# Causal attention and maxout FFN on one core: the written engine order becomes a priority

## The chip, the cores and the metric

The kernel runs on one core of a Trainium2 chip. The time is device microseconds of that core for one execution; before the change it is 972.1 us (median of 3 runs, 967.75 to 972.37). Five engines work side by side: TensorE (PE, with its weight loads as PEld), VectorE (DVE), ScalarE (ACT), GpSimd (POOL) and SyncE (SP, which here only issues DMAs). Each has one queue of instructions, fixed when the program is built, and an instruction waits at the head of its queue until the semaphores that it needs are there.

## The reference

The kernel computes causal attention with a decay bias for 8 batches of 8 heads (576 positions, head size 64), and then a feed-forward layer with a maximum over three up-projections:

```
scores = q @ k.T / sqrt(64)
cum    = cumsum(max(s, 0))
scores = where(causal, -1e9, scores + min(-(cum_q - cum_k), 0))
attn   = exp(scores - max(scores));  attn = attn / (sum(attn) + 1e-9)
x      = (attn @ v)                      # to 4608 tokens x 512
h      = max(x @ w1, x @ w2, x @ w3)     # 512 -> 768
out    = h @ w_out                       # 768 -> 512
```

The weights arrive as 64-bit floats and are decoded in the kernel. Products that need more than half precision are done as sums of parts: a high and a low part of each operand, three matmuls in place of one.

## The kernel before, in words

**Attention.** Heads are taken in pairs; a pair of one batch is a *visit*, and a block of 128 queries of a visit is a *step*. Batches 0 and 1 are visited twice, first for query blocks 0 and 1, then for blocks 2 to 4; batches 2 to 7 are visited once, for all five. That makes 160 steps. One step `t` goes through four functions, each on other engines:

- `scores(t)` (L359): PE writes the scores of both heads into a PSUM tile `s`. There are two such tiles (L64), so step `t+2` needs the tile of step `t` back.
- `highest(t)` (L445): DVE takes the row maximum `nm`.
- `expo(t)` (L451): ACT takes the exponential in place and the row sums `se`.
- `probs(t)` (L466): DVE takes the reciprocal `ri` (L480), ACT writes the high part `prh` (L496), DVE the low part `prl` (L499), which is the last reader of the score tile; then SP issues the transposing DMAs of both parts (L502, or L508 and L512 for the last block).

`values(v, ph)` (L534) multiplies the transposed probabilities with V on PE once the blocks 0 and 1 (`ph` 0) or 2 to 4 (`ph` 1) of a visit are done; its result goes to the tiles `x` (ACT L562, DVE L563).

**FFN.** When four visits have filled the `x` of one batch and half, `add_set` (L665) queues 18 groups `h_group` (12 matmuls each, L679, three of them per block of 128 hidden units) and 4 groups `o_group` (18 matmuls each, L721). A group accumulates in one of three PSUM tiles `m` (L66). The first product of a block is copied out by ACT (L693), the other two are maximised into it by DVE (L696); then ACT (L685) and POOL (L686) split it into `hh` and `hl`.

**Preparation.** Heads are loaded by SP (L121) and split into high and low parts (L150 to L168), V is scaled and split (L346, L351). The 24 weight tiles are loaded, decoded on ACT and DVE (`decode1`, `decode2`, L589 to L593), measured with small matmuls (`gram1`, L603), and then written as half-precision parts (`decode3` L647, `decode4` L652). The scale of the up weights needs all 18 of them, so the FFN can't begin before that.

**What sets the order.** The Python program emits all of this in one order. The main loop (L877 to L905) is a software pipeline by hand: in the round of step `t` it emits `probs(t)` in two parts, `highest(t+1)` between them, at most one FFN group, `scores(t+2)`, `expo(t+1)`, then what the tables `todo` and `early` hold for this step (loads, preparation, decoding), more FFN groups, and the `values` of the step before. How many groups a round takes is set by a budget: each step adds `STEP_NS` = 4800 ns less the step's own PE cost (L878), and each group takes off its cost (L752). Evacuations of a group are held back in `pending` and `later` until `drain` and `flush`.

All of it stands inside `manual_schedule()` (L67): every engine issues its instructions in exactly the order in which the program emits them. Tile buffers are handed out in that order too. The program is built with `schedule_with_timeline_sim=True` (L965).

Of the kernel before, what the change touches and what calls it, by code (L numbers as in the profile page):

```python
# [21 lines left out]
def kernel(  # L22
# [41 lines left out]
    ps_s = ctx.enter_context(tc.tile_pool(name="ps_s", bufs=2, space=PSUM))  # L64
    ps_av = ctx.enter_context(tc.tile_pool(name="ps_av", bufs=1, space=PSUM))
    ps_m = ctx.enter_context(tc.tile_pool(name="ps_m", bufs=3, space=PSUM))  # L66
    ctx.enter_context(tc.manual_schedule())  # L67


    visits = [(b, g, qbs) for qbs in ((0, 1), (2, 3, 4)) for b in range(NB) for g in range(NP)]  # L70
# [898 lines left out]
```

## Time and profile before

| | before |
|---|---|
| time, median of 3 runs | 972.1 us |
| span of the profiled execution (first to last instruction) | 972.4 us |
| highest of the three runs | 972.37 us |
| PE busy | 847.3 us, 87% |
| ACT busy | 599.1 us, 62% |
| DVE busy | 589.2 us, 61% |
| POOL busy | 285.2 us, 29% |
| mean granted clock of PE | 0.944 of full speed |

The profiled execution spans 972.4 us, and its own time is that of the highest of the runs shown, 972.37 us: nothing measurable lies around the span. Busy shares are means over a long ramp, a steady stretch and a tail that have different limits, so the prediction reads them by stage. A row of the views of waits names the instruction that waited, what released it, the microseconds in total, how often and the longest. In a timeline the number in brackets is how long the engine had been idle before the instruction, and who released it.

### The profile page before, as it was taken

What the parts mean: (1) busy time and instruction counts of PE and PEld (TensorE: products, weight loads), DVE (VectorE), ACT (ScalarE), POOL (GpSimd) and SP (SyncE); (2) the same over time, 40 slices, a digit from 0 to 9 for tenths busy, and PEclk for the clock granted to TensorE, in tenths of its full rate; (3) what the DMA queues carried; (4) which work ended last, traced back from release to release, by engine and by line L of the source; (5) the groups of instructions that cost most, each with busy time, mean ns of one, the idle gap of its engine ahead of it and who ended that gap; (6) DMA issues with size and microseconds to landing.
All of it is one profiled execution on the core that took longest, in us unless ns stands there. A gap on an engine that the chain in (4) does not pass through costs nothing. (4 is left out here: it accounts for less than half of the span.)

```text
span 972.4 us, 19924 instructions
## 1 busy us (share of the span) xinstructions
PE 847.3 (87%) x7192; PEld 658.6 (68%) x7192; DVE 589.2 (61%) x1216; ACT 599.1 (62%) x1598; POOL 285.2 (29%) x455
## 2 busy tenths in 40 slices
PE   2547759997889967999999998999999999999998
PEld 2435547775557746876788777877787778777876
DVE  6898876656546665656666566665666666554111
ACT  4657566565547676676667676666676676765121
POOL 2001221212333432333333433444343433320101
PEclk9756979999889978999999999999999999999999
DMA  8952245477467777676868676875867776734000
GB/s 299 261 149 61 82 89 128 109 134 141 93 134 145 132 159 134 126 151 117 155 115 151 120 159 111 151 140 121 150 114 143 130 156 115 140 66 97 5 24 28
DMA packets 242035, 122.34 MB, mean 126 GB/s; under 512 B 217808, under 2 KB 226512, under 8 KB 241936
## 3 DMA queue, kind: packets, MB, share of 16 engines
q1 hardware_dynamic: 237904, 108.74, 56.8%
q10 hardware_dynamic: 4032, 12.32, 4.1%
q8 instruction: 57, 0.93, 0.4%
q14 instruction: 42, 0.34, 0.2%
HBM read 60.18 MB, written 9.44 MB: 72 GB/s over the span
## 5 line engine op out<-in xcount | busy, mean ns | idle before, releaser
L679 PE MATMUL pm<-x,w 128*128 128x256 f16 (+1 forms) x3456 | 461.0, 290 | 10.9 <-DVE x L563 5.6
L679 PEld LDWEIGHTS <-w 128*128 128x128 f16 x3456 | 335.0, 99 | 99.3 <-issue 11.5
L499 DVE SCALAR_TENSOR_TENSOR prl<-s,ri,prh 128x512 f16<-128x512 f32 (+3 forms) x288 | 153.0, 568 | 109.4 <-ACT prh L496 75.5
L686 POOL TENSOR_TENSOR hl<-m,hh 128x256 f16<-128x256 f32 (+1 forms) x96 | 73.9, 770 | 459.8 <-ACT hh L685 429.8
L496 ACT ACTIVATE prh<-s,ri 128x512 f16<-128x512 f32 (+3 forms) x288 | 141.6, 538 | 41.5 <-DVE ri L480 31.3
L457 ACT ACTIVATE s<-s,nm 128x512 f32<-128x512 f32 (+4 forms) x288 | 150.9, 524 | 9.7 <-DVE nm L447 5.5
L721 PE MATMUL po<-hh,w 128*128 128x256 f16 (+1 forms) x768 | 153.0, 290 | 3.1 <-ACT hh L685 3.0
L696 DVE SCALAR_TENSOR_TENSOR m<-pm,m 128x256 f32<-128x256 f32 (+1 forms) x192 | 87.2, 454 | 106.3 <-PE pm L679 91.7
L447 DVE TENSOR_REDUCE nm<-s 128x1 f32<-128x576 f32 (+4 forms) x160 | 127.7, 798 | 37.0 <-PE s L382 24.4
L721 PEld LDWEIGHTS <-w 128*128 128x128 f16 x1152 | 111.9, 99 | 33.7 <-issue 5.5
L721 PE MATMUL po<-hl,w 128*128 128x320 f16 (+1 forms) x384 | 111.2, 290 | 1.6 <-POOL hl L686 1.6
L685 ACT ACTIVATE hh<-m 128x256 f16<-128x256 f32 (+1 forms) x96 | 42.3, 440 | 105.3 <-DVE m L696 105.3
L562 ACT ACTIVATE x<-av 128x256 f16<-128x256 f32 (+1 forms) x64 | 26.3, 411 | 78.4 <-PE av L552 78.3
L693 ACT ACTIVATE m<-pm 128x256 f32<-128x256 f32 (+1 forms) x96 | 38.9, 405 | 52.6 <-PE pm L679 52.4
L168 POOL TENSOR_TENSOR l<-raw,h 64x576 fp32r<-64x576 f32 x48 | 67.9, 1414 | 2.3 <-ACT h L154 0.7
L376 PE MATMUL s<-h 128*128 128x128 f32 (+1 forms) x192 | 54.9, 368 | 15.1 <-DVE prl L499 11.8
L563 DVE SCALAR_TENSOR_TENSOR x<-av,x 128x256 f16<-128x256 f32 (+1 forms) x64 | 29.1, 454 | 64.1 <-ACT x L562 64.1
L137 POOL CAST l<-kb 64x576 fp32r<-64x576 f32 x48 | 31.9, 666 | 113.0 <-PE s L391 100.7
L552 PEld LDWEIGHTS <-vh 128*64 128x64 f16 x832 | 45.0, 114 | 22.3 <-issue 13.4
L552 PE MATMUL av<-ph,vh 128*64 128x320 f16 (+3 forms) x384 | 57.9, 293 | 2.3 <-DMA ph<-prh 2.3
L729 ACT ACTIVATE o<-po,os 128x256 f32<-128x256 f32 (+1 forms) x64 | 31.9, 498 | 45.1 <-PE po L721 28.6
L552 PE MATMUL av<-pl,vh 128*64 128x320 f16 (+3 forms) x384 | 57.1, 285 | 2.8 <-DMA pl<-prl 2.5
(138 smaller groups left out, 1108.8 us busy)
## 6 DMA issues: line engine op xcount, KB each, us to landing
raw<-in_qk_dram SPq DMA_DIRECT2D x96, 304.0 KB, 4.8
r<-in_w_dram ACTq DMA_DIRECT2D x20, 512.0 KB, 4.8
rv<-in_qkv_dram SPq DMA_DIRECT2D x32, 320.0 KB, 3.3
out_dram<-o SPq DMA_DIRECT2D x32, 160.0 KB, 2.2
out_dram<-o SPq DMA_DIRECT2D x32, 128.0 KB, 2.2
raw<-in_qkv_dram SPq DMA_DIRECT2D x8, 480.0 KB, 3.8
ph<-prh SPq DMA_TRANSPOSE x192, 3.3
pl<-prl SPq DMA_TRANSPOSE x192, 2.8
```

The lines of the kernel that those rows point to most:

```text
L168: nc.gpsimd.tensor_tensor(out=l[far, QP:V0], in0=raw[far, QP:V0], in1=h[far, QP:V0].bitcast(F32), op=ALU.subtract)
L376: nc.tensor.matmul(ps[:, j, :nk], lhsT=w[:, qs], rhs=w[:, QP:QP + nk], start=(x == "h"), stop=False, skip_group_check=True,)
L447: nc.vector.tensor_reduce(out=nm, in_=sc, axis=AX.X, op=ALU.max, negate=True)
L457: nc.scalar.activation(out=sc, in_=sc, func=AF.Exp, bias=nm[:, j:j + 1], accum_out=sm[:, j:j + 1])
L496: nc.scalar.activation(out=hi, in_=src, func=AF.Copy, scale=sc)
L499: nc.vector.scalar_tensor_tensor(out=lo, in0=src, scalar=sc, in1=hi, op0=ALU.mult, op1=ALU.subtract)
L552: nc.tensor.matmul(av[j * D:(j + 1) * D, c0:nq], lhsT=lt, rhs=rt, start=(n < 2), stop=(n >= len(todo) - 2), skip_group_check=True,)
L679: nc.tensor.matmul(pm[:, :nq], lhsT=w[:, wt, kt, :], rhs=xt, start=(n == 0), stop=(n == 3 * NKT - 1))
L685: nc.scalar.activation(out=st["hh"][:, ft, :nq], in_=m1[:, :nq], func=AF.Copy)
L686: nc.gpsimd.tensor_tensor(out=st["hl"][:, ft, :nq], in0=m1[:, :nq], in1=st["hh"][:, ft, :nq], op=ALU.subtract)
L696: nc.vector.scalar_tensor_tensor(out=m1[:, :nq], in0=pm[:, :nq], scalar=HSC, in1=m1[:, :nq], op0=ALU.mult, op1=ALU.max)
L721: nc.tensor.matmul(pm[:, :nq], lhsT=W[18 + ft][:, wt, dt, :], rhs=st[ht][:, ft, :nq], start=(n == 0), stop=(n == 3 * NFT - 1),)
```

## The change

One line goes:

```diff
--- before.py
+++ after.py
@@ -64,7 +64,6 @@
     ps_s = ctx.enter_context(tc.tile_pool(name="ps_s", bufs=2, space=PSUM))
     ps_av = ctx.enter_context(tc.tile_pool(name="ps_av", bufs=1, space=PSUM))
     ps_m = ctx.enter_context(tc.tile_pool(name="ps_m", bufs=3, space=PSUM))
-    ctx.enter_context(tc.manual_schedule())
```

No operation is added or removed, no shape, engine or buffer count changes, and the Python program emits the same instructions in the same order. What changes is what the order means. Without the region, the framework's scheduler plays the program through against its own model of the engines' times; whenever an engine is free in that model, it takes the earliest emitted instruction whose inputs are there and whose output tile has a free buffer. The outcome is again one fixed order for each engine, with semaphores between them. On the chip, an engine still can't pass over an instruction that waits.

This holds for all queues: the matmuls on PE, the elementwise work on DVE, ACT and POOL, and the DMA issues on SP and on ACT (L186, L96, L111).

## The prediction

> **What bounds the kernel now.** I read the page first, then the busy time by stage, then PE's waits in each stage, because a mean over 972 us hides three limits.
>
> ```profile
> span 972.4 us, 19924 instructions
> PE 847.3 (87%) x7192; PEld 658.6 (68%) x7192; DVE 589.2 (61%) x1216; ACT 599.1 (62%) x1598; POOL 285.2 (29%) x455
> PEclk9756979999889978999999999999999999999999
> ```
>
> ```profile
> core 0: us, PE busy (x) PEld busy (x) DVE busy (x) ACT busy (x) POOL busy (x), PEclk, DMA share, GB/s
> 0.00:80.00 80.00, 34.64 (x256) 27.29 (x257) 64.63 (x154) 45.09 (x128) 10.87 (x36) 0.74 0.74 221
> 80.00:160.00 80.00, 61.23 (x514) 48.12 (x512) 64.37 (x127) 53.30 (x133) 14.00 (x16) 0.83 0.35 83
> 160.00:410.00 250.00, 214.29 (x1770) 161.82 (x1770) 148.69 (x295) 156.56 (x408) 75.68 (x113) 0.92 0.68 133
> 410.00:893.00 483.00, 463.53 (x4064) 363.30 (x4063) 299.10 (x614) 328.82 (x896) 175.32 (x276) 1.00 0.69 130
> 893.00:972.00 79.00, 73.58 (x594) 58.05 (x593) 12.40 (x28) 15.36 (x35) 9.29 (x14) 0.98 0.10 25
> ```
>
> PE is idle 45.4 us in the ramp (80 less 34.64), 18.8 in the second stage, 35.7 in the third, 19.5 in the steady stretch and 5.4 in the tail: 125 us in all. In the ramp DVE is the busy engine (64.63 of 80). From 410 us on PE is, at 96% and at full clock. What PE waits for there and in the third stage (the waits of PE alone, first from 160 to 410 us, then from 410 to 893 us):
>
> ```profile
> PE s L436 <- DVE prl L499: 13.4, 5, 4.3
> PE s L391 <- DVE prl L499: 7.0, 3, 3.6
> PE s L376 <- DVE prl L499: 2.8, 3, 1.9
> ```
>
> ```profile
> PE s L376 <- DVE prl L499: 9.1, 14, 1.0
> PE pm L679 <- DVE x L563: 4.7, 4, 1.2
> PE s L391 <- DVE prl L499: 4.1, 4, 1.0
> PE av L552 <- DMA pl<-prl: 0.3, 1, 0.3
> ```
>
> One wait leads everywhere: scores of step t+2 wait for the low part of step t, the last reader of the score tile. In the steady stretch it shows 18 times, 13.2 us together, 0.73 us each, and never longer than 1.0. The rows below (groups of DVE, then one of ACT, in this stretch alone; the last numbers before the second bar are busy us and mean ns) say that it has 95 steps (the reciprocal is one per step), so a step takes 483/95 = 5.08 us and four steps in five show no such wait.
>
> ```profile
> L696 DVE SCALAR_TENSOR_TENSOR m<-pm,m 128x320 f32<-128x320 f32 (+1 forms) x109 | 49.8, 457 | 41.0 <-PE pm L679 31.2 <-POOL hl L686 4.2 <-issue 2.6
> L159 DVE SCALAR_TENSOR_TENSOR h<-raw,h 64x640 fp32r<-64x640 f32 x35 | 31.1, 890 | 0.6
> L351 DVE SCALAR_TENSOR_TENSOR vl<-rv,inv,vh 128x640 f16<-128x640 f32 x19 | 20.4, 1072 | 0.0
> L480 DVE RECIPROCAL ri<-se 128x2 f32<-128x2 f32 (+1 forms) x95 | 15.1, 159 | 33.2 <-ACT se L461 32.5
> ```
>
> **The change part by part.** Nothing is removed or added, so busy time stays: PE has 847 us of work in either order. The sum is over PE's idle time by stage, and it is made against the profiled execution's 972.4 us, which is 0.3 us over the median of the runs.
>
> *Ramp, 0 to 80 us.* The FFN waits for the up weights, and those for DVE. Being free to pass over a waiting instruction helps here. The timeline of DVE and ACT around the first split weights:
>
> ```profile
> 74.24 0.40 DVE L447 TENSOR_REDUCE nm<-s 128x2 f32<-128x256 f32 x1
> 74.29 2.03 ACT L647 ACTIVATE w<-r,swu 128x512 f16<-128x512 f32 x3 [2.30 <-DVE swu L629]
> 77.62 0.88 DVE L499 SCALAR_TENSOR_TENSOR prl<-s,ri,prh 128x256 f16<-128x256 f32 x2 [2.98 <-ACT prh L496]
> ```
>
> DVE stands 2.98 us for a low part of a step, while the first high parts of the weights are being written and their low parts (L652) could follow. More than DVE's idle time in the stage, 15.4 us, can't be won; less than nothing only if decoding gets in front of attention, which then has no PE work to give up (PE is 43% busy). Bounds -15 and +3, and I take -5: that one wait of 3.0, and some 2 us of the decoding that can fill other holes.
>
> *80 to 410 us.* PE idles 54.5 us here, 23.2 of it in the three rows of waits above. In the written order an FFN group can't pass a score matmul that waits; in the new one it can. But groups are there only when a set of x is complete, and a group taken early is missing in the next hole, so most of it moves the hole. Bounds -33 (the 23.2 and five lost clocks of 2.0, below) and +24 (a wait of the steady kind, 0.73 us, at each of the 65 steps before 410 us, which are 160 less 95, is 47, less the 23.2 there). I take -10, on the side of the three rows.
>
> *Steady stretch, 410 to 893 us.* Here there is little to win (19.5 us idle) and a cover to lose. The written order puts a whole group between the release of a score tile and the scores that use it (`run_group` at L889 ahead of `scores` at L893); 12 matmuls take 1.8 us by a row below. The scheduler keeps no such distance: scores are emitted ahead of later groups, so they are taken the moment the tile is free in its model, and on the chip PE stands wherever the real chain is later than the modelled one. The chain gets later too. DVE and ACT are 62% and 68% busy in this stretch; when the next link of a step isn't there yet, they now start whatever is ready, and a link that comes in meanwhile waits for its end. Fillers on DVE last 0.457 (L696), 0.890 (L159) and 1.072 us (L351), mean 0.81, so half of one is 0.40 us on average, at two links of a step on DVE (the reciprocal and the low part), and at one link on ACT, where the filler in the row of L150 lasts 0.726 us, 0.36. That is 1.16 us a step, 110 us over 95 steps, if nothing hides it. Behind a late link stand the low part, the transposes and the scores of step t+2; the group's 1.8 us hid them. Bounds: -19 (all idle time gone) to +110. The nearest row is the wait of 0.73 us: if it comes in three steps of four, as against one in five now, it is 95 x 0.75 x 0.73 = 52 us, less the 13.2 already there: +39. I take +39.
>
> *DMA issues.* They are moved as well, on SP's queue and ACT's. The issue times of SP (source rows of L502 and L121, min/median/max in ns):
>
> ```profile
> L502 SPq DMA_TRANSPOSE ph<-prh x128: 1168/1222/2484, 18.3 to 891.2; - x128
> L502 SPq DMA_TRANSPOSE pl<-prl x128: 1167/1232/3192, 19.7 to 892.7; - x128
> L121 SPq DMA_DIRECT2D raw<-in_qk_dram x96: 471/582/1992, 234.2 to 844.3; - x96
> ```
>
> A visit of five steps has 13 transposes and 4 head loads: 13 x 1.23 + 4 x 0.58 = 18.3 of 25.4 us, 72% of the queue before the other issues. A load that is now issued as soon as its buffer is free may stand ahead of a transpose and delay it by 0.58 us. What hides that is the round between the last transpose and `values` (5.08 us; PE waited 0.3 us for it). Without that cover it would be 2 x 0.58 us for each of 19 visits, 22 us. I take nothing, and keep it for the range. Weight loads on ACT's queue lie in the ramp, where the DMA engines are 74% busy.
>
> *Tail, 893 to 972 us.* Attention is over and the groups follow each other; nothing competes, so 0.
>
> Sum: 972.4 - 5 - 10 + 39 = 996.4. I say **997 us**.
>
> **The clock.** Short waits do not cost more than themselves at present, long ones do (timeline of PE):
>
> ```profile
> 224.56 3.42 PE L679 MATMUL pm<-x,w 128*128 128x320 f16 x24
> 237.52 1.79 PE L679 MATMUL pm<-x,w 128*128 128x320 f16 x12
> 243.57 0.55 PE L436 MATMUL s<-qkh 128*128 128x256 f32 x1 [4.26 <-DVE prl L499]
> 245.72 5.41 PE L679 MATMUL pm<-x,w 128*128 128x320 f16 x24
> ```
>
> After a gap of 4.26 us the same 24 matmuls take 5.41 us in place of 3.42: 2.0 us more. In the steady stretch no wait passes 1.2 us and the granted clock is 1.00.
>
> The Trainium skill ("TensorE: Matmul & The Clock Gate", section "Why this matters for your kernels") puts the limit at idle gaps of about 3 us, past which the clock halves. By that rule my 0.73 us waits leave the clock alone and the sum stays; it speaks against the change only if an order of the model's own makes gaps of the ramp's size in the steady stretch, which is the fifth case below. The row agrees with the rule for 4.26 us; no run here yet shows a gap near 3.
>
> **The rivals.**
>
> *Faster: the holes fill and the cover stays (945 us).* Place: ramp and third stage. The model's PE is then as full as the chip's, so that ready work of earlier emission always goes first and the order in the steady stretch stays as written. Price: -5 in the ramp and the 23.2 us of score waits from 160 to 410 us: 972.4 - 28 = 944, say 945. It decides if the score waits of the steady stretch stay near 13 us; once they pass 13 + 28 = 41 us, it has lost. For it: 96% busy PE leaves little that could be passed over. Against it: the groups that fill a hole were already budgeted for the next. Chance 0.24.
>
> *No change (972 us).* Where instructions are nearly always ready in the order in which they are emitted, the scheduler gives back the written order, and the line does nothing. ACT and DVE, a third idle, speak against it. Chance 0.11.
>
> *Work far ahead takes a buffer (1036 us).* The three PSUM tiles `m` serve groups, weight measurements and scales alike, and slots of raw weights are used again for `x` and heads. An engine with nothing ready (POOL is 29% busy) may open a late tile early, and the earlier user of the slot then waits. An FFN set that is pushed behind attention costs its time in the tail, by the chain that ended last:
>
> ```profile
> 929.78 29.34 PE pm L679 x216
> 959.12 9.79 PE po L721 x72
> ```
>
> That is 39.1 us on top of the forecast: 997 + 39 = 1036. For it: one buffer per slot of the weights. Against it: earlier emission still wins whenever both are ready. Chance 0.12.
>
> *The clock falls in the steady stretch (1076 us).* If each of the 19 visits there gets one gap of the length in the timeline above, it costs 4.26 + 2.0 = 6.3 us, 119 in all: 972.4 - 15 + 119 = 1076. For it: the gap of 4.26 us has the very cause that the change touches, a score tile that comes back late. Against it: no wait of the steady stretch is over 1.2 us, and a ready group can fill a hole. Chance 0.05.
>
> **How the numbers follow.** The forecast, 997 us, is the likeliest single case, with 0.48. Its own range is 978 to 1025: the wait of 0.73 us in two steps of four gives 972.4 - 15 + 35 - 13 = 979, in every step 972.4 - 15 + 69 - 13 = 1013, and half of the 22 us of SP's uncovered delays goes on top. The whole range goes from 940, a little under the faster case, to 1045, a little over the buffer case; outside stay the case of the clock, and the ends of the two cases next to the bounds, under 2 in 10 together. A change of under 0.5% can't be told from none here. Faster by more than that has the 0.24 of its case, within it the 0.11 of the case of no change, and slower 0.48 + 0.12 + 0.05 = 0.65.
>
> **What would show it.** In the changed profile the first FFN matmul (L679; at about 80 us now) should come up to 5 us earlier. Between 160 and 410 us the waits of PE for `prl` should shrink below 23 us. In the steady stretch PE's waits for `prl` L499 should grow from 13 us to about 52, in many short waits of under 3 us, with the share of PE busy falling from 96% to about 89% and the clock staying at 1.00. The tail should be the same length. I am wrong if the steady stretch keeps its 19 us of idle time (then the faster case holds, and the cover is not what the order gave), if the loss sits before 160 us (then decoding or a buffer held by late work is the cause, and the first term has the wrong sign), or if it sits in `values`, as waits for the transposes (then SP's order counts, which I set to nothing).

## The result, and the profile after

The changed kernel takes 995.1 us (median of 4 runs, 993.86 to 996.32) against 972.2 us before (4 runs, 967.75 to 973.4). The ratio is 1.0236, with a 95% interval of 1.0205 to 1.0267: slower by some 23 us, where 25 were forecast. Each run also gave its span: 993.8 us for the one of 995.62 us, so 1.8 us lie around a span, and not nothing as written above the prediction. One line went from the file, so each line number below is one less than in the kernel before.

Two lines of the page of the changed kernel, and its busy time in the stages of the prediction:

```profile
span 993.8 us, 20079 instructions
PE 858.9 (86%) x7192; PEld 655.8 (66%) x7192; DVE 579.4 (58%) x1216; ACT 594.4 (60%) x1598; POOL 302.2 (30%) x455
```

```profile
core 0: us, PE busy (x) PEld busy (x) DVE busy (x) ACT busy (x) POOL busy (x), PEclk, DMA share, GB/s
0.00:80.00 80.00, 32.49 (x209) 21.73 (x209) 61.49 (x157) 39.80 (x106) 13.40 (x37) 1.00 0.64 214
80.00:160.00 80.00, 66.42 (x582) 51.43 (x581) 61.37 (x128) 59.53 (x158) 20.83 (x27) 0.94 0.46 105
160.00:410.00 250.00, 214.90 (x1773) 161.07 (x1772) 147.86 (x302) 155.47 (x410) 79.75 (x113) 0.95 0.67 130
410.00:893.00 483.00, 448.06 (x3831) 346.30 (x3831) 283.49 (x578) 309.11 (x847) 177.84 (x265) 0.99 0.63 124
893.00:993.00 100.00, 96.99 (x809) 75.22 (x805) 25.21 (x56) 30.53 (x79) 10.34 (x14) 1.00 0.21 44
```

The PEclk of 1.00 in the first row is no reading of the ramp: the trace's record of the clock begins at 85 us here, at 35 us before. PE idles 34.9 us in the steady stretch (483 less 448.06), where it was 19.5. The same stretch of time holds less work: 3831 matmuls, before 4064. Over the whole span PE's idle time grew by 9.9 us and its busy time by 11.6 (858.9 less 847.3), with the same matmuls. The place of the loss is seen best by milestones. The table gives, from the traces, when the reciprocal of a step starts (us), which every step has once; two of the experiments below stand beside it.

| step | before | after | written from step 40 | pinned preparation |
|---|---|---|---|---|
| 20 | 154.9 | 153.7 | 154.1 | 156.6 |
| 40 | 284.1 | 272.2 | 271.1 | 265.9 |
| 60 | 385.6 | 378.5 | 371.7 | 364.4 |
| 70 | 437.3 | 436.6 | 424.0 | 413.9 |
| 100 | 591.9 | 603.7 | 580.8 | 563.4 |
| 140 | 798.1 | 824.9 | 789.9 | 762.7 |
| 159 | 892.9 | 918.8 | 886.1 | 858.1 |
| end | 972.4 | 993.8 | 966.3 | 933.1 |

So the free order wins 12 us by step 40, has given them back by step 70, loses a further 27.4 us by step 140 (0.39 us a step), and regains some 4 us in the tail.

What PE waits for between 410 and 893 us in the changed kernel:

```profile
PE pm L678 <- ACT o L728: 14.1, 6, 3.4
PE s L375 <- DVE prl L498: 5.9, 5, 2.0
PE av L551 <- DMA pl<-prl: 5.1, 7, 1.4
PE s L390 <- DVE prl L498: 2.5, 3, 1.1
PE pm L678 <- DVE m L695: 2.1, 5, 0.7
PE s L375 <- DVE tl L498: 2.0, 1, 2.0
```

The score waits, which were to grow to 52 us, are down to 10.4 (5.9 + 2.5 + 2.0; 13.2 before). New is the first row: groups wait for a PSUM tile `m` that ACT has not yet copied out, 14.1 us in six waits. What keeps ACT is seen in one of them (a few rows of three timelines; `...` marks rows left out). The first fence is ACT's timeline, the second SP's, the third PE's:

```profile
590.54 0.24 ACT L456 ACTIVATION_READ_ACCUMULATOR s<-s,nm 128x1 f32 x1
593.93 0.74 ACT L149 ACTIVATE h<-raw 128x640 fp32r<-128x640 f32 x1 [3.16 <-DMA raw<-in_qk_dram]
594.58 0.67 ACT L153 ACTIVATE h<-raw 128x576 fp32r<-128x576 f32 x1
595.15 1.25 ACT L495 ACTIVATE prh<-s,ri 128x512 f16<-128x512 f32 x2
596.29 0.53 ACT L728 ACTIVATE o<-po,os 128x320 f32<-128x320 f32 x1
```

```profile
588.38 1.18 SPq L120 DMA_DIRECT2D raw<-in_qk_dram  x2
```

```profile
591.73 1.91 PE L678 MATMUL pm<-x,w 128*128 128x256 f16 x16
...
596.87 3.42 PE L678 MATMUL pm<-x,w 128*128 128x256 f16 x16 [3.23 <-ACT o L728]
```

ACT stands 3.16 us at the split of a head (L149) whose load SP issued between 588.4 and 589.6. Behind it in ACT's queue stands the copy of `o` (L728), though its input is long there (PE's last matmul for it ends at 591.0); PE then waits 3.23 us for that PSUM tile, and the 16 matmuls after that gap take 3.42 us where 16 took 1.91 ahead of it. Over the whole span such standing adds up (waits of ACT and DVE, first after, then before):

```profile
ACT h L149 <- DMA raw<-in_qk_dram: 49.2, 24, 4.7
DVE am L288 <- DMA rv<-in_qkv_dram: 68.4, 27, 6.3
DVE h L158 <- ACT h L149: 30.5, 15, 4.5
```

```profile
ACT h L150 <- DMA raw<-in_qk_dram: 9.7, 3, 6.9
DVE am L289 <- DMA rv<-in_qkv_dram: 1.5, 1, 1.5
```

117.6 us at loads, where the written order had 11.2. The scheduler lets the preparation start as soon as its load has landed in its model. On the chip a head load lands 4.6 us after its issue (median on the page; 4.8 before), a V load 4.3 (3.3 before), and in these 51 places the engine came to the preparation before that. For the last 28 loads of V the maximum (L288) starts in the median 4.4 us after the load's issue, at the moment of its landing; before, it was 7.1 us after the issue, 3.7 us after the landing. That the model has the loads land earlier than the chip is inferred from this; no trace shows the model's own times.

### The profile page after: what moved, and what is told of

Same layout as the page of the kernel before. It is cut to its first block, busy times and chain, and to the rows that moved or that the text cites. A ratio compares the mean times of both kernels' runs of the same rounds, so it can differ in the third digit from the quotient of the medians.

```text
span 993.8 us, 20079 instructions
## 1 busy us (share of the span) xinstructions
PE 858.9 (86%) x7192; PEld 655.8 (66%) x7192; DVE 579.4 (58%) x1216; ACT 594.4 (60%) x1598; POOL 302.2 (30%) x455
## 5 line engine op out<-in xcount | busy, mean ns | idle before, releaser
L678 PE MATMUL pm<-x,w 128*128 128x256 f16 (+1 forms) x3456 | 466.7, 291 | 29.4 <-ACT o L728 14.1
L678 PEld LDWEIGHTS <-w 128*128 128x128 f16 x3456 | 336.1, 100 | 123.2 <-issue 34.9
L685 POOL TENSOR_TENSOR hl<-m,hh 128x256 f16<-128x256 f32 (+1 forms) x96 | 71.1, 741 | 307.1 <-ACT hh L684 300.9
L551 PEld LDWEIGHTS <-vh 128*64 128x64 f16 x832 | 50.3, 112 | 39.5 <-issue 23.1
L551 PE MATMUL av<-ph,vh 128*64 128x320 f16 (+3 forms) x384 | 63.8, 289 | 12.2 <-DMA ph<-prh 7.9
L551 PE MATMUL av<-pl,vh 128*64 128x320 f16 (+3 forms) x384 | 63.6, 283 | 9.8 <-DMA pl<-prl 9.5
L167 POOL TENSOR_TENSOR l<-raw,h 64x576 fp32r<-64x576 f32 x48 | 71.7, 1493 | 0.0
L479 DVE RECIPROCAL ri<-se 128x2 f32<-128x2 f32 (+1 forms) x160 | 25.3, 161 | 74.7 <-ACT se L460 74.0
L288 DVE TENSOR_REDUCE am<-rv 128x1 f32<-128x640 f32 (+1 forms) x36 | 27.7, 774 | 68.5 <-DMA rv<-in_qkv_dram 68.4
L158 DVE SCALAR_TENSOR_TENSOR h<-raw,h 64x640 fp32r<-64x640 f32 x48 | 49.2, 1025 | 31.3 <-ACT h L149 30.5
L149 ACT ACTIVATE h<-raw 128x640 fp32r<-128x640 f32 x48 | 35.3, 736 | 49.8 <-DMA raw<-in_qk_dram 49.2
```

Source lines behind the costliest of these rows:

```text
L158: nc.vector.scalar_tensor_tensor(out=h[own, 0:QP], in0=raw[own, 0:QP], scalar=SCALE, in1=h[own, 0:QP].bitcast(F32), op0=ALU.mult, op1=ALU. ...
L167: nc.gpsimd.tensor_tensor(out=l[far, QP:V0], in0=raw[far, QP:V0], in1=h[far, QP:V0].bitcast(F32), op=ALU.subtract)
L551: nc.tensor.matmul(av[j * D:(j + 1) * D, c0:nq], lhsT=lt, rhs=rt, start=(n < 2), stop=(n >= len(todo) - 2), skip_group_check=True,)
L678: nc.tensor.matmul(pm[:, :nq], lhsT=w[:, wt, kt, :], rhs=xt, start=(n == 0), stop=(n == 3 * NKT - 1))
L685: nc.gpsimd.tensor_tensor(out=st["hl"][:, ft, :nq], in0=m1[:, :nq], in1=st["hh"][:, ft, :nq], op=ALU.subtract)
```

## The experiments

Theories: **A**, ACT and DVE stand at preparations whose loads land later than modelled. **B**, the prediction's: PE's own order takes scores up too early. **C**, SP's order makes the transposes late. Each run is compared with runs of the kernel before on the same chip (medians 972.0 to 973.1 us); brackets hold the 95% interval of the ratio.

### One engine's order at a time

In place of the removed line, the region is kept for some engines:

```diff
-    ctx.enter_context(tc.manual_schedule())
+    ET = mybir.EngineType
+    ctx.enter_context(tc.manual_schedule(engines={ET.Activation, ET.DVE, ET.Pool, ET.SP}))
```

With this set PE's order is the scheduler's. For ACT and DVE free the set is PE, Pool and SP; for SP free it is PE, Activation, DVE and Pool.

> Only PE's order is left to the scheduler; ACT, DVE, POOL and SP keep the written order. Theory A (the loss sits in ACT's and DVE's order: they stand at a preparation whose load has not landed, and the copies out of the PSUM tiles m queue behind it): the loss is gone, 965 to 976 us. Theory B (the prediction's: PE's own order takes scores up too early and stands at them): 985 to 1000 us, with PE's waits for prl in the steady stretch well over 13 us. Theory C (SP's order makes the transposes late): 965 to 976 us as in A.

Measured: 1014.5 us, 1.0453 [1.0401, 1.0504].

> Only ACT's and DVE's orders are left to the scheduler; PE, POOL and SP keep the written order. Theory A: most of the loss is here, 985 to 1000 us, with ACT's waits for the head loads well over the 9.7 us of before and PE waiting for the tiles m. Theory B: 965 to 978 us. Theory C: 965 to 978 us.

Measured: 1023.0 us, 1.0514 [1.0478, 1.0550].

> Only SP's order (its DMA issues) is left to the scheduler. Theory A: 968 to 976 us, as the engines that compute keep the written order. Theory B: 968 to 976 us. Theory C: 980 to 1000 us, with PE's waits for the transposes above 6 us in the steady stretch.

Measured: 965.5 us, 0.9927 [0.9901, 0.9953].

Theory C is out: a free SP wins 6.5 us, which no theory had forecast. Theory A and theory B each got a loss where they wanted one, larger than their ranges, and each a loss where they wanted none; either set alone loses more than all engines together. So these three runs decide nothing between A and B. PE alone does not lose by B's wait, though: from 410 to 893 us it waits 12.1 us for low parts (4.4 for `prl`, 7.7 for `tl`; 13.2 before). In that stretch (PE free, then before) PE's scores come late for DVE, which is the other direction:

```profile
DVE nm L448 <- PE s L383: 100.8, 48, 5.0
```

```profile
DVE nm L447 <- PE s L382: 13.7, 15, 1.5
```

With ACT and DVE free, in the same stretch:

```profile
ACT h L151 <- DMA raw<-in_qk_dram: 32.6, 17, 4.0
```

```profile
PE po L722 <- ACT hh L686: 12.5, 8, 2.8
PE pm L680 <- ACT x L563: 6.4, 4, 2.0
PE pm L680 <- DVE x L564: 5.2, 4, 1.5
```

Here PE, in its written order, waits for copies and splits of ACT and DVE, which fits A.

### The written order from step 40 on

```diff
     for t, (v, qb) in enumerate(steps):
+        if t == 40:
+            ctx.enter_context(tc.manual_schedule())
```

> The written order begins at step 40 (about 275 us); everything emitted before is the scheduler's. In the changed kernel step 40 comes 12 us earlier than before, and the loss builds up after step 60. If the two stretches are independent (theories A and B alike), the lead stays: 957 to 965 us. If the lead is only work taken from later steps, it is given back at the seam: 969 to 976 us.

Measured: 961.7 us, 0.9878 [0.9846, 0.9909]. The lead at step 40 holds to the end in most part, 10.4 us of it by the medians. (The profiled run in the table, 968.1 us, is the slowest of the four, with a granted clock of 0.95 in the steady stretch; the others took 958.1 to 963.8.) At step 70 this kernel is still 13.2 us ahead of before, the changed one 0.6. So nothing was borrowed, and the loss belongs to the free order after step 40.

The same with SP left to the scheduler throughout (`engines={PE, Activation, DVE, Pool}` in that region):

> From step 40 on PE, ACT, DVE and POOL follow the written order and SP stays with the scheduler; before step 40 all is the scheduler's. If the 6.5 us that a free SP won are others than the lead at step 40: 951 to 957 us. If they are the same (in the run with a free SP alone they appear between steps 30 and 40): 957 to 964 us.

Measured: 959.9 us, 0.9868 [0.9836, 0.9900]. A free SP adds little on top (1.7 us, within the noise): its gain looks like part of the same lead.

### Without the loads

```diff
 def load_head(v, j):
+        if v > 2 * NP * NB:
+            R.setdefault(v, {})["raw", j] = R[2 * NP * NB]["raw", j]
+            return
...
 def load_v(v, dma=None):
+        if v >= 2 * NP * NB + NP:
+            R.setdefault(v, {})["rv"] = R[v - NP]["rv"]
+            return
```

Left out are 92 of the 96 transfers of heads and 20 of the 32 transfers of V of 320 KB. By the edit it is batches 3 to 7 that use the V of batch 2, not 4 to 7 that of batch 3 as the expectation says.

> Leaves out loads: visits 17 and later use the heads of visit 16 again, and batches 4 to 7 the V of batch 3, so no preparation on ACT, DVE and POOL waits for a load in the steady stretch; the arithmetic is all done. Written order. The trace of before shows 9.7 us of ACT's waits for head loads, so 960 to 972 us under every theory; it is the base for the next two.

Measured: 965.1 us, 0.9923 [0.9900, 0.9946].

> The same loads left out, order by the scheduler on all engines. Theory A (ACT and DVE stand at preparations whose load lands later than modelled): the distance to the written order with the same loads left out shrinks from 23 us to under 10. Theory D (the orders fail at any wait, loads or not): it stays at 18 to 28 us.

Measured: 946.9 us, 0.9729 [0.9704, 0.9754]: 18 us *below* the written order without those loads, where it was 23 above with them. The swing of 41 us is larger than A's own forecast. PE's busy time and all its waits in the steady stretch of this run:

```profile
410.00:893.00 483.00, 481.18 (x4232) 379.54 (x4231) 291.21 (x595) 329.28 (x899) 184.91 (x271) 1.00 0.40 77
```

```profile
PE po L726 <- ACT o L734: 1.0, 5, 0.2
PE av L557 <- DMA tT<-tl: 0.4, 1, 0.4
PE av L557 <- DMA ph<-prh: 0.4, 1, 0.4
```

The preparation is not held back here and still runs in full; its waits at loads of heads and V are down to 16.4 us over the whole span (3.6 on ACT and 12.8 on DVE).

> The same loads left out, only ACT's and DVE's orders left to the scheduler. With the loads this kernel is 51 us above before. Theory A: the distance to the written order with the same loads left out falls to under 25 us. Theory D: it stays over 40 us.

Measured: 991.9 us, 1.0184 [1.0142, 1.0226], 26.8 us over the written order without loads. The loss has halved (51 with loads), but it is not under the 25 that A set; something beside the loads costs a free ACT and DVE against a written PE.

> Loads left out as in the two runs above, only PE's order left to the scheduler (with the loads that was 42 us above before). If the loads are the cause there too, because the model has them land earlier and lays PE's order on that: under 975 us, near the 965 of the written order with the same loads left out. If PE's order alone is at odds with the written order of the others whatever the loads do: 995 to 1015 us.

Measured: 1003.7 us, 1.0328 [1.0273, 1.0383], 38.6 us over the written order without loads, about as much as with them. For PE alone the loads are not the cause. In both cases a scheduled order on some engines beside a written order on the others loses time without these loads too; why, these runs don't settle.

### The loads kept, the preparation held back

This is the test that A could still lose, since leaving loads out also takes work from SP and the DMA engines. All engines stay with the scheduler and all loads are made, but in ACT's and DVE's queues the preparation may not stand ahead of the last exponential sums and low parts emitted before it. This is an order on one engine's queue, not a wait:

```diff
-        nc.scalar.activation(out=se[:, :nj], ...)
+        LAST["a"] = nc.scalar.activation(out=se[:, :nj], ...).ins
...
-            nc.vector.scalar_tensor_tensor(out=lo, in0=src, ...)
+            LAST["v"] = nc.vector.scalar_tensor_tensor(out=lo, in0=src, ...).ins
...
         for f, a in todo.get(t, ()):
-            f(*a)
+            with ExitStack() as pin:
+                if f in (head_qhi, head_khi, head_qlo, vmax):
+                    for x in "av":
+                        pin.enter_context(tc.issue_after(LAST[x]))
+                f(*a)
```

> All engines stay with the scheduler and all loads are done; but the preparation of the heads (L150, L154, L159 of before and the POOL work behind them) and the maximum of V (L289) may not stand ahead of the exponential sums and low parts of the step at which the written program emits them. Theory A: ACT and DVE no longer stand at loads, and the changed kernel's loss goes: 945 to 972 us, with ACT's waits for head loads under 15 us (49.2 in the changed kernel). Theory C' (what the left out loads took from SP's queue and the DMA engines was the gain, not the waits): it stays at 985 to 1000 us.

Measured: 936.5 us (934.9 to 938.12), 0.9635 [0.9582, 0.9688]: 59 us below the changed kernel and some 36 below the kernel before, the fastest of all. Theory C' is out. Its waits at loads over the whole span (ACT, then DVE), and its steady stretch, with all that PE waits for in it:

```profile
ACT h L149 <- DMA raw<-in_qk_dram: 1.1, 1, 1.1
```

```profile
DVE am L288 <- DMA rv<-in_qkv_dram: 0.2, 1, 0.2
```

```profile
410.00:854.00 444.00, 441.72 (x3855) 344.79 (x3854) 282.29 (x583) 310.79 (x851) 170.17 (x262) 1.00 0.71 133
```

```profile
PE pm L683 <- ACT m L697: 1.8, 4, 0.5
```

The waits at loads are gone, 117.6 to 1.3 us, and PE is busy 99.5% until attention is nearly over (441.72 of 444), with the DMA engines as busy as before (0.71, before 0.69). It no longer waits for a score tile there at all.

The two halves of it alone, `(head_qhi, head_khi)` and then `(vmax,)` in the list of functions:

> As before, but only ACT's part of the head preparation (L150 and L154) is held back; the low parts and the maximum of V are the scheduler's. Theory A: the waits of DVE for V loads (68 us in the changed kernel) stay, those of ACT for head loads go; 950 to 985 us, and not faster than the run with all of it held back.

Measured: 979.4 us, 1.0074 [1.0050, 1.0098]. As A has it, the waits for V stay, those for heads go (1.1 us), and it is slower than with all held back:

```profile
DVE am L288 <- DMA rv<-in_qkv_dram: 73.8, 27, 6.4
```

> The counterpart of the run that held back ACT's head preparation alone (979 us): only the maximum of V on DVE (L289) is held back to its written step, the head preparation is the scheduler's. If the waits for V loads are the larger part of the loss: 940 to 965 us. If those for head loads are as large, so that each alone still leaves the other: 970 to 990 us, with ACT's waits for head loads over 30 us.

Measured: 962.3 us, 0.9871 [0.9838, 0.9903], with ACT's waits for the head loads still there. The time is that of the first branch, the waits are those of the second:

```profile
ACT h L149 <- DMA raw<-in_qk_dram: 45.7, 22, 4.5
```

Holding V's maximum back is worth 33 us (995.1 to 962.3), the ACT part of the heads 16 (to 979.4), and both, with the heads' low parts on DVE, 59. The 10 us beyond the sum of the two are not split up between the low parts and the two acting together. An instruction of 0.8 us on DVE that nobody was in a hurry for was the larger half of what could be won; the links of every step stand behind it in DVE's queue. Against the run with all held back, a microsecond stood at loads costs the kernel somewhat over half a microsecond in each of the halves (43 us for 73.8, 26 for 45.7) and half a one in the changed kernel (59 for 117.6).

## Why the prediction was right, and where it was not

The time is right to 2 us: 995.1 measured, 997 forecast. That is in part luck. In the spans, the changed kernel is 4.0 us ahead at step 65 (near 410 us), where -15 was forecast; it loses 29.9 us from there to step 159, where +39 was forecast; and the tail wins 4.4, where nothing was forecast. The misses cancel, and the largest term is there for another reason than the one given.

**Ramp, -5.** Not so: the first FFN matmul starts at 80.7 us, before at 80.0. By step 20 the kernel is 1.2 us ahead. In between the free order put decoding in front of attention, which the prediction had as its risk: step 10 comes at 104.2 us, before at 83.4, and the low parts of the up weights are all written by 96 us, before by 122.

**80 to 410 us, -10.** Right up to step 40, where the lead is 11.9 us, and the hybrid with the written order from there on shows that this is a true gain. Between steps 20 and 40 PE idles 6.4 us less (12.9 for 19.3) and its work takes 4.3 us less (105.6 for 109.9, at a granted clock of 0.99 for 0.93). PE's waits for `prl` from 160 to 410 us fall as foreseen, from 23.2 to 7.9 us. But the rest of the stage gives most of it back, down to 4.0 us at step 65: PE's idle time from 160 to 410 us is 35.1 us, before 35.7, so most holes moved, as the prediction itself feared.

**Steady stretch, +39.** This is the step that failed. "A cover to lose" was the argument: scores taken up the moment that the tile is free, PE standing there in three steps of four, 52 us of score waits. They fell, from 13.2 to 10.4 us. The pinned kernel keeps no written distance either, and PE waits for no score tile in its steady stretch: the cover was not what the order gave. By the prediction's own condition, score waits near 13 us, the faster case should have held. It did not, because PE's waits for the tiles `m` rose from nothing to 17.3 us and those for transposes from 0.3 to 6.4. What was missing is a wait that the prediction looked at in DMA issues only from the sending side. It asked what a load pulled forward does to a transpose behind it, and not what the user of the load does when it, too, is pulled forward: it is put where the load is about to land, on an in-order queue with the evacuations behind it. Holding four functions back, with every load still made, takes these waits from 117.6 to 1.3 us and removes the whole loss, so this is shown. The size, 29.9 for 39, came near by luck: the price was that of another wait.

**Busy time.** "PE has 847 us of work in either order" did not hold: PE is busy 858.9 us in the changed kernel and 844.6 in the pinned one. So part of the loss shows as longer matmuls and not as waits; the clock below accounts for some 5 us in the steady stretch, the rest is open.

**Fillers.** The thought that a link of the chain waits for whatever was started ahead of it was right in kind. (Its 0.726 us on ACT is the mean of L150 in the steady stretch, 25.4 us over 35; that row does not stand in the fence.) But the prediction let a filler start only when it was ready. The order is fixed when the program is built, and on the chip the engine stands at a filler whose load is missing: 2.3 us on average in the 51 places, 6.3 at most, against 0.8 for running it. The runs without the loads tell the two apart: there the fillers run ahead just as freely, with 16.4 us of standing, and the free order takes 946.9 us.

**DMA issues, 0.** Left to the scheduler alone, SP wins 6.5 us, of which 5.0 are there at step 40. The waits of PE for transposes in the steady stretch, 6.4 us in the changed kernel, are gone in the pinned one, where SP is just as free; so SP's order alone did not make them.

**Clock.** The gap of 3.23 us above slowed the next 16 matmuls from 1.91 to 3.42 us, 1.5 us more. The Trainium skill ("TensorE: Matmul & The Clock Gate", section "Why this matters for your kernels") names gaps over about 3 us as what brings the clock down; the rows here agree only in part. Of the four longest gaps of the steady stretch, all waits for L728, the one above and the last below were followed by slow matmuls, the other two were not (24 of these matmuls take 2.78 us at full clock):

```profile
485.70 2.78 PE L678 MATMUL pm<-x,w 128*128 128x256 f16 x24 [3.04 <-ACT o L728]
707.89 2.78 PE L678 MATMUL pm<-x,w 128*128 128x256 f16 x24 [3.39 <-ACT o L728]
818.10 4.45 PE L678 MATMUL pm<-x,w 128*128 128x256 f16 x24 [2.97 <-ACT o L728]
```

So a gap near 3 us may or may not be paid once more. The mean granted clock of the stretch is 0.99, which is some 5 us of the 483 (an estimate from these two numbers). The prediction's "no run here yet shows a gap near 3" overlooked its own row of L391, with a wait of 3.6 us.

**The other rivals.** The order did change, so the case of no change is out. No late tile that took a buffer shows in the waits of the steady stretch, and the tail is shorter, not longer (75.0 us from the last reciprocal to the end, 79.5 before).

Open: why a free order on PE alone, or on ACT and DVE alone, costs more than on all engines, loads or not.

## What to carry to other kernels

Where a scheduler orders in-order queues by a model, look for every instruction whose input comes by DMA: it may be placed so close behind the issue of its load that the engine stands at it, and then all that is queued behind it stands too, however unimportant the instruction itself is. Tie such users to the step at which they are needed, and leave the rest free; here that beat both the written order and the free one, 936.5 us against 972 and 995. Cost a moved transfer at both ends, where it is issued and where it is used.

## What was not expected of the hardware

An engine's share of busy time says little of what its standing costs: DVE is busy 58% in the changed kernel, and 68 us of waits at a maximum that the written program emits 3 to 16 steps ahead of its reader cost the kernel some 33 us. And PE can be kept busy 99.5% of 444 us at the full granted clock (1.00) with 133 GB/s of DMA traffic beside it; the 4% idle of the written order were no floor.
